# A two-step pipeline, a convolution in 64x64 array tiles, and casts moved between engines, in a fused attention and feed-forward kernel

## The chip, the core and the metric

One core of a Trainium2 chip. The metric is device microseconds of one execution; most executions of a kernel agree within 0.3%, some are 1.5% or more slower and are called slow. The engines are TensorE (PE; PEld is its weight load), VectorE (DVE), ScalarE (ACT), GpSimd (POOL) and SyncE (SP), which issues the transfers. SBUF is the on-chip memory that holds the tiles, PSUM the one that TensorE writes its results to. "Span" is what the profile of one execution covers.

## The reference, cut to what matters

```python
for t in range(S):                                  # B=4, H=8, S=768, D=48
    cur = einsum(u * k_t, v_t)
    y_t = einsum(r_t, state + cur)
    state = w * state + einsum(k_t, v_t)
x = y as (B, S, 384)
gate = sigmoid(sum over 5 taps of conv_w[tap] * shifted x)   # per channel, causal
out = (gate * (x @ w_val)) @ w_out
```

Attention is done in chunks of 128 positions with decays multiplied into k and r beforehand. A **unit** is two chunks (256 positions of one batch), so there are 12 units.

## The kernel before

Each unit goes through: transposes of scaled k and r; `prod` (the product pr of rT and kT on VectorE), `bonus` (a small matmul giving s), scores and mask, state and decay, `bonus_v` (dv = v * s on GpSimd); then the attention output `y_out`, and the feed-forward: `conv`, `value`, `project`. The loop runs them four steps deep:

```python
for i in range(N + 3):
    x, a, y, f = i, i - 1, i - 2, i - 3
    ... loads for x + 3
    if ok(a): prod(a)
    if ok(f): conv(f)
    if ok(x): transp_k(x)
    if ok(a): bonus(a); attn(a, 0); mask_at(a, 0); bonus_v(a); state(a, 0); decay(a, 0)
    if ok(f): value(f)
    if ok(a): attn(a, 1); mask_at(a, 1); state(a, 1); decay(a, 1)
    if ok(y): y_out(y)
    if ok(f): project(f)
    ...  # two of the next batch's r pieces in two steps of three: scale_r on GpSimd, transp_r
    if ok(x + 1) and x > 0: scale_k(x + 1)          # on VectorE
    if ok(x + 1): cast_v(x + 1)                     # two casts on GpSimd
```

The convolution uses full 128x128 diagonal weights, one per tap and per 128 channels:

```python
for Ts in ((0, 1), (2,)):
    g_ps = ps_mm.tile([128, len(Ts), W], F32, name="mm_ps")      # ps_mm: three PSUM buffers
    for i, T in enumerate(Ts):
        for t in range(KW):                                       # 5 taps, W = 256 columns
            nc.tensor.matmul(out=g_ps[:, i, :], lhsT=cwdiag[:, T, t, :],
                             rhs=xT[:, T, t0 + t : t0 + t + W], start=(t == 0), stop=(t == KW - 1))
    nc.scalar.activation(out=gate[...], in_=g_ps, func=AF.Sigmoid)
```

## Time and profile before

| | before |
|---|---|
| time, median of 4 runs | 122.94 us (122.79 to 123.26) |
| span of the profiled run | 123.1 us; that run took 124.88 us, a slow one |
| steps from one attention output to the next, in the steady part | 7.45 us on average |
| TensorE busy between the outputs of units 2 and 9 | 51.8 of 52.2 us |

Lines of the profile give start, duration, engine, line, operation, output and inputs, and in brackets what ended the idle time before. The product pr:

```profile
45.55 0.69 DVE L259 TENSOR_TENSOR pr<-rT,kT 128x1024 bf16<-128x1024 bf16 x1 [2.13 <-ACT rT L222]
52.02 0.68 DVE L259 TENSOR_TENSOR pr<-rT,kT 128x1024 bf16<-128x1024 bf16 x1
59.28 0.99 DVE L259 TENSOR_TENSOR pr<-rT,kT 128x1024 bf16<-128x1024 bf16 x1
```

It takes 0.69 us, once 0.99.

### The profile page before, as it was taken

The page shows a single profiled execution, that of the slowest core. Times are in us where ns is not written, and L with a number is a line of the kernel's source. Part 1 is how long each engine was busy: PE and PEld are TensorE (multiplying, and loading weights), DVE is VectorE, ACT ScalarE, POOL GpSimd, SP SyncE. Part 2 cuts the span into 40 slices and gives each one's busy share as a digit, 9 for nine tenths or more (in the row PEclk, how much of TensorE's full clock was granted, in tenths as well). Part 3 has the DMA queues.
Part 4 walks back from the last instruction along what each step waited for, and adds up shares of the span by engine and source line. Part 5 has one row for each costly group of instructions (what it writes and reads, how often), then busy time and mean ns, then how long its engine had stood idle before and what let it go on. Part 6 is the DMA issues. An engine that isn't in the chain of part 4 may idle for free.

```text
span 123.1 us, 4291 instructions
## 1 busy us (share of the span) xinstructions
PE 100.1 (81%) x1851; PEld 77.7 (63%) x1851; DVE 81.7 (66%) x130; ACT 65.4 (53%) x113; POOL 62.3 (51%) x84
## 2 busy tenths in 40 slices
PE   0035862893589999999999999999999999999950
PEld 0023641672357687886977878787787877778720
DVE  0549669663856938959597695986949787653030
ACT  4599720319033393664938737295691736364730
POOL 6926516592817927039789430995946050500000
PEclk9999999999555799999999999999999999999999
DMA  2999999997999989688499779782030110303213
GB/s 46 166 339 233 193 206 347 242 319 142 221 213 243 326 173 252 136 204 179 141 290 258 183 168 239 151 191 74 5 128 5 61 67 5 128 8 133 74 54 128
DMA packets 58510, 20.54 MB, mean 167 GB/s; under 512 B 50422, under 2 KB 58491, under 8 KB 58491
## 3 DMA queue, kind: packets, MB, share of 16 engines
q1 hardware_dynamic: 58362, 20.26, 67.0%
q8 instruction: 14, 0.23, 0.8%
q0 software_dynamic: 128, 0.00, 0.2%
q14 instruction: 6, 0.04, 0.1%
HBM read 15.54 MB, written 4.72 MB: 165 GB/s over the span
## 4 chain that ended last, share of the span: by engine, by line
PE 63%; SPq 17%; DVE 8%; DMA 5%; issue 2%; ACT 1%; DVEq 0%
PE mm_ps L397 16%; PE mm_ps L359 11%; SPq L72 10%; PE mm_ps L437 10%; PE mm_ps L417 8%; DMA k_st<-in_k_dram 5%; SPq L80 5%; PE at_ps L293 5%; PE tr_ps L246 4%; PE kv_ps L319 3%; DVE cwdiag L197 3%; PE tr_ps L221 3%; DVE at L305 2%; PE kv_ps L328 2%; PE mm_ps L266 2%
## 5 line engine op out<-in xcount | busy, mean ns | idle before, releaser
L279 POOL TENSOR_TENSOR dv<-v_st,s_sb 128x384 bf16<-128x384 f32 x24 | 19.4, 828 | 31.3 <-PE at_ps L293 27.9
L305 DVE TENSOR_TENSOR at<-at_ps,mask 128x1024 bf16<-128x1024 f32 x24 | 29.3, 1220 | 2.6 <-PE at_ps L293 1.6
L387 ACT CAST xT<-mm_ps 128x384 bf16<-128x384 f32 x24 | 11.5, 478 | 31.1 <-PE mm_ps L359 30.4
L397 PE MATMUL mm_ps<-xT,cwdiag 128*128 128x256 bf16 x180 | 23.4, 284 | 1.5 <-DVE cwdiag L197 1.5
L238 POOL CAST vb<-v_st 128x384 bf16<-128x384 f32 x24 | 17.6, 753 | 9.0 <-DMA v_st<-in_v_dram 9.0
L397 PEld LDWEIGHTS <-cwdiag 128*128 128x128 bf16 x180 | 17.6, 100 | 5.5 <-DVE cwdiag L197 2.4
L209 POOL TENSOR_TENSOR rs<-r_st,dr 128x576 bf16<-128x576 f32 x13 | 18.6, 1449 | 3.5 <-DMA r_st<-in_r_dram 3.4
L246 PE MATMUL tr_ps<-ident,ks 128*128 128x128 bf16 x96 | 9.0, 250 | 10.1 <-DVE ks L228 9.9
L425 DVE TENSOR_TENSOR hT<-mm_ps,gate 128x512 bf16<-128x512 f32 (+1 forms) x24 | 12.2, 548 | 7.2 <-PE mm_ps L417 7.2
L249 ACT COPY kT<-tr_ps 128x1024 bf16<-128x1024 bf16 x12 | 12.1, 1012 | 7.8 <-PE tr_ps L246 7.3
L404 ACT ACTIVATE gate<-mm_ps 128x512 bf16<-128x512 f32 (+1 forms) x24 | 11.2, 493 | 8.6 <-PE mm_ps L397 6.8
L228 DVE TENSOR_TENSOR ks<-k_st,dk 128x768 bf16<-128x768 f32 x12 | 13.2, 1098 | 3.5 <-DMA k_st<-in_k_dram 3.5
L417 PE MATMUL mm_ps<-xT,wval 128*128 128x256 bf16 x108 | 14.7, 284 | 0.0
L246 PEld LDWEIGHTS <-ks 128*128 128x128 bf16 x96 | 7.6, 113 | 11.1 <-DVE ks L228 10.6
L437 PE MATMUL mm_ps<-wout,hT 128*128 128x384 bf16 x72 | 13.8, 328 | 0.5 <-DVE hT L425 0.5
L444 ACT COPY o_sb<-mm_ps 128x384 f32<-128x384 f32 x24 | 11.5, 478 | 3.0 <-PE mm_ps L437 1.8
L222 ACT COPY rT<-tr_ps 128x768 bf16<-128x768 bf16 x16 | 12.1, 808 | 0.4 <-PE tr_ps L221 0.4
L293 PE MATMUL at_ps<-rT,kT 48*128 48x128 bf16 x192 | 10.8, 239 | 1.7 <-DVE at L305 1.5
L259 DVE TENSOR_TENSOR pr<-rT,kT 128x1024 bf16<-128x1024 bf16 x12 | 8.8, 735 | 5.0 <-ACT rT L222 5.0
L417 PEld LDWEIGHTS <-wval 128*128 128x128 bf16 x108 | 10.8, 102 | 2.0 <-issue 0.2
L344 DVE TENSOR_TENSOR z<-kv_ps,wcm 128x384 bf16<-128x384 f32 x20 | 10.9, 547 | 0.0
L275 DVE COPY s_sb<-mm_ps 128x16 f32<-128x16 f32 x12 | 2.1, 174 | 12.5 <-issue 5.2
(58 smaller groups left out, 125.6 us busy)
## 6 DMA issues: line engine op xcount, KB each, us to landing
k_st<-in_k_dram SPq DMA_DIRECT2D x24, 192.0 KB, 4.7
r_st<-in_r_dram SPq DMA_DIRECT2D x8, 576.0 KB, 6.2
v_st<-in_v_dram SPq DMA_DIRECT2D x24, 192.0 KB, 4.5
out_dram<-o_sb SPq DMA_DIRECT2D x12, 384.0 KB, 2.6
wv_st<-in_moe_w_val_dram SPq DMA_DIRECT2D x1, 576.0 KB, 4.8
wo_st<-in_moe_w_out_dram SPq DMA_DIRECT2D x1, 576.0 KB, 6.0
w_bc<-in_w_dram SPq DMA_DIRECT2D x1, 192.0 KB, 3.7
wt<-in_w_dram POOLq DMA_DIRECT2D x2, 0.8 KB, 4.5
```

The source lines that it names most:

```text
L72: nc.sync.dma_start(out=d[n][:, cl], in_=src[b, :, t0 : t0 + C, :].transpose([1, 0, 2]))
L209: eng.tensor_tensor(out=rs_t[p][:, :, :, 0:D].rearrange("p j a d -> p a j d"), in0=r_st[b][:, hs, :].rearrange("p a (j d) -> p a j d", d=D ...
L228: nc.vector.tensor_tensor(out=ks_t[n % 3][:, :, :, :, 0:D].rearrange("p c n a d -> p c (n a) d"), in0=k_st[n], in1=dk[:, None, :, :].to_br ...
L238: nc.gpsimd.tensor_copy(heads(vb[:, cl], H), v_st[n][:, cl])
L246: nc.tensor.transpose(tr[:, cl, p, :], ks[:, cl, p].rearrange("p a x -> p (a x)"), ident)
L279: nc.gpsimd.tensor_tensor(out=dv_t[n % 2][:, cl].rearrange("p (h d) -> p h d", d=D), in0=v_st[n][:, cl], in1=st["s", n][:, cl, :, None].to ...
L293: nc.tensor.matmul(out=at_ps[:, par, p, :], lhsT=kT[rows, p, cs], rhs=rT[rows, p, cs], start=(p == 0), stop=(p == NP - 1), skip_group_chec ...
L305: nc.vector.tensor_tensor(out=st["at", n, cl].rearrange("p a n i -> p (a n) i"), in0=st["at_ps", n, cl].rearrange("p a n i -> p (a n) i"), ...
L359: nc.tensor.matmul(out=y_ps[32 * q : 32 * q + 32, T, :], lhsT=lt, rhs=rh, start=q not in first, stop=last, skip_group_check=True,)
L397: nc.tensor.matmul(out=g_ps[:, i, :], lhsT=cwdiag[:, T, t, :], rhs=xT[:, T, t0 + t : t0 + t + W], start=(t == 0), stop=(t == KW - 1),)
L417: nc.tensor.matmul(out=v_ps[:, i, :], lhsT=wval[:, kt, T * 128 : T * 128 + 128], rhs=xT[:, kt, t0 : t0 + W], start=(kt == 0), stop=(kt == ...
L437: nc.tensor.matmul(out=o_ps, lhsT=hT[:, T, cl * C : cl * C + C], rhs=wout[:, T, :], start=(T == 0), stop=(T == NT - 1),)
```

## The change

Intent: shorten the start and the drain of the pipeline (feed-forward one step behind the scores instead of two), cut TensorE's convolution by packing four 64x64 tiles into the array, and take the k scaling off VectorE and the v casts off GpSimd. Its core:

```diff
-    for i in range(N + 3):
-        x, a, y, f = i, i - 1, i - 2, i - 3
+    for i in range(N + 1):
+        f = i - 1
...
+        if ok(f): y_out(f)
+        if ok(i + 1):
+            cast_v(i + 1)                     # now one cast on ScalarE
+            scale_k(i + 1, nc.gpsimd)         # was on VectorE
+        if ok(i):
+            prod(i); attn(i, 0); mask_at(i, 0)
+            bonus(i); bonus_v(i); state(i, 0); decay(i, 0)
+        ... scale_r on GpSimd, one or two pieces
+        if ok(f): conv(f); value(f)
+        if ok(i): attn(i, 1); mask_at(i, 1); state(i, 1); decay(i, 1)
+        ... transp_r, transp_k(i + 1), project(f), transp_r
```

```diff
-                        lhsT=cwdiag[:, T, t, :],
-                        rhs=xT[:, T, t0 + t : t0 + t + W],
+        for T0 in (0, 2):
+            for t in range(KW):
+                for q in range(2):
+                    for i in range(2):
+                        T = 2 if T0 else i
+                        c0, n0, o0 = (i * C, C, W) if T0 else (0, W, 0)
+                        rows = slice(64 * q, 64 * q + 64)
+                        qo = (q + i) % 2
+                        nc.tensor.matmul(
+                            out=g_ps[i][64 * qo : 64 * qo + 64, o0 : o0 + n0],
+                            lhsT=cwdiag[rows, T, t, :],
+                            rhs=xT[rows, T, t0 + c0 + t : t0 + c0 + t + n0], ...)
```

Cut away here: value, projection and weights follow the new layout of the channels; the first batch's r is loaded and scaled ahead of everything (two pieces on GpSimd); 60 warm-up matmuls run ahead; the diagonals are prepared at the end of step 0; the last output goes out in two halves.

More of the change, by code (lines that the diff above doesn't have):

```diff
@@ L77, in load_r @@
         r_st[b] = ldr.tile([128, H, J * D], F32, name="r_st")
-        for hh in range(2):
-            hs = slice(hh * NP, hh * NP + NP)
+        nd = NP if b == 0 else 2
+        for hh in range(nd):
+            hs = slice(hh * (H // nd), (hh + 1) * (H // nd))
             nc.sync.dma_start(
@@ L86 @@
     nc.sync.dma_start(out=w_bc, in_=w.partition_broadcast(128))
-    load_kv(0, "k")
     load_r(0)
+    load_kv(0, "kv")
     load_kv(1, "k")
-    load_kv(0, "v")
-    load_kv(2, "k")
-    load_kv(1, "v")
     nc.scalar.preload_act_table_set("natural_log_exp_and_others")
@@ L172 @@
     wv_st = consts.tile([128, NT, DM], F32)
-    wo_st = consts.tile([128, NT, DM], F32)
+    wo_st = consts.tile([128, 4, DM], F32)
     cw5 = consts.tile([KW, DM], F32)
@@ L178, in load_weights @@
         nc.sync.dma_start(out=wv_st, in_=moe_w_val.rearrange("(t p) n -> p t n", p=128))
-        nc.sync.dma_start(out=wo_st, in_=moe_w_out.rearrange("(t p) n -> p t n", p=128))
-    wval = consts.tile([128, NT, DM], BF16)
-    wout = consts.tile([128, NT, DM], BF16)
+        wo = moe_w_out.rearrange("(t p) n -> p t n", p=128)
+        nc.sync.dma_start(out=wo_st[:, 0::2, :], in_=wo[:, 0::2, :])
+        nc.sync.dma_start(out=wo_st[64:128, 1::2, :], in_=wo[0:64, 1:3, :])
+        nc.sync.dma_start(out=wo_st[0:64, 1::2, :], in_=wo[64:128, 1:3, :])
+    wval = consts.tile([128, NT, 4, 128], BF16)
+    wout = consts.tile([128, 4, DM], BF16)
     cw5b = consts.tile([KW, DM], BF16)
     cwT = consts.tile([128, NT, KW], F32)
-    cwdiag = consts.tile([128, NT, KW, 128], BF16)
+    cwdiag = consts.tile([128, NT, KW, 64], BF16)
+    eye = consts.tile([128, 64], BF16)
     def prep_conv():
@@ L194, in prep_conv, with cast_weights @@
         nc.vector.tensor_copy(cwT, cw_ps[:, :, 0:KW])
-    def prep_diag(T):
-        nc.vector.tensor_tensor(
-            out=cwdiag[:, T],
-            in0=ident[:, None, :].to_broadcast([128, KW, 128]),
-            in1=cwT[:, T, :, None].to_broadcast([128, KW, 128]),
-            op=ALU.mult,
-        )
+        for q in range(2):
+            rows = slice(64 * q, 64 * q + 64)
+            nc.vector.tensor_copy(eye[rows], ident[rows, rows])
+        for T in range(NT):
+            nc.vector.tensor_tensor(
+                out=cwdiag[:, T],
+                in0=eye[:, None, :].to_broadcast([128, KW, 64]),
+                in1=cwT[:, T, :, None].to_broadcast([128, KW, 64]),
+                op=ALU.mult,
+            )
+    def cast_weights():
+        wv = wv_st.rearrange("p k (t x) -> p k t x", x=128)
+        nc.gpsimd.tensor_copy(wval[:, :, 0::2, :], wv[:, :, 0::2, :])
+        nc.gpsimd.tensor_copy(wval[:, :, 1::2, 64:128], wv[:, :, 1:3, 0:64])
+        nc.gpsimd.tensor_copy(wval[:, :, 1::2, 0:64], wv[:, :, 1:3, 64:128])
+        nc.scalar.copy(out=wout, in_=wo_st)
     st = {}
@@ L214, in scale_r, with transp_r @@
         )
-    def transp_r(b, p):
+    def transp_r(b, p, dve=False):
         if p == 0:
@@ L221, in transp_r @@
             nc.tensor.transpose(tr[:, j, :], rs_t[p][:, j].rearrange("p a x -> p (a x)"), ident)
-        nc.scalar.copy(
+        (nc.vector.tensor_copy if dve else nc.scalar.copy)(
             out=st["rT", b][:, p, :].rearrange("x (p j) -> x p j", j=J),
@@ L225, in transp_r, with scale_k @@
         )
-    def scale_k(n):
-        nc.vector.tensor_tensor(
+    def scale_k(n, eng):
+        eng.tensor_tensor(
             out=ks_t[n % 3][:, :, :, :, 0:D].rearrange("p c n a d -> p c (n a) d"),
@@ L236, in cast_v @@
         vb = vb_t[n % 4]
-        for cl in range(U):
-            nc.gpsimd.tensor_copy(heads(vb[:, cl], H), v_st[n][:, cl])
+        nc.scalar.copy(
+            out=vb[:, :, 16 : 16 + 64 * H].rearrange("p c (h x) -> p c h x", x=64)[:, :, :, 0:D],
+            in_=v_st[n],
+        )
     def transp_k(n):
@@ L277, in bonus_v @@
     def bonus_v(n):
-        for cl in range(U):
-            nc.gpsimd.tensor_tensor(
-                out=dv_t[n % 2][:, cl].rearrange("p (h d) -> p h d", d=D),
-                in0=v_st[n][:, cl],
-                in1=st["s", n][:, cl, :, None].to_broadcast([128, H, D]),
-                op=ALU.mult,
-            )
+        nc.gpsimd.tensor_tensor(
+            out=dv_t[n % 2].rearrange("p c (h d) -> p (c h) d", d=D),
+            in0=v_st[n].rearrange("p c h d -> p (c h) d"),
+            in1=st["s", n].rearrange("p c h -> p (c h)")[:, :, None].to_broadcast([128, U * H, D]),
+            op=ALU.mult,
+        )
     def attn(n, cl):
@@ L391, in conv @@
         xT, t0 = xT_t[b % 2], cu * W
-        gate = ffn.tile([128, NT, W], BF16, name="gate")
-        for Ts in ((0, 1), (2,)):
-            g_ps = ps_mm.tile([128, len(Ts), W], F32, name="mm_ps")
-            for i, T in enumerate(Ts):
-                for t in range(KW):
-                    nc.tensor.matmul(
-                        out=g_ps[:, i, :],
-                        lhsT=cwdiag[:, T, t, :],
-                        rhs=xT[:, T, t0 + t : t0 + t + W],
-                        start=(t == 0),
-                        stop=(t == KW - 1),
-                    )
-            nc.scalar.activation(
-                out=gate[:, Ts[0] : Ts[-1] + 1, :], in_=g_ps, func=AF.Sigmoid
-            )
+        gate = ffn.tile([128, 2, W + C], BF16, name="gate")
+        g_ps = [ps_mm.tile([128, W + C], F32, name="mm_ps") for i in range(2)]
+        for T0 in (0, 2):
+            for t in range(KW):
+                for q in range(2):
+                    for i in range(2):
+                        T = 2 if T0 else i
+                        c0, n0, o0 = (i * C, C, W) if T0 else (0, W, 0)
+                        rows = slice(64 * q, 64 * q + 64)
+                        qo = (q + i) % 2
+                        nc.tensor.matmul(
+                            out=g_ps[i][64 * qo : 64 * qo + 64, o0 : o0 + n0],
+                            lhsT=cwdiag[rows, T, t, :],
+                            rhs=xT[rows, T, t0 + c0 + t : t0 + c0 + t + n0],
+                            start=(t == 0 and T0 == 0),
+                            stop=(t == KW - 1),
+                            skip_group_check=True,
+                        )
+        for i in range(2):
+            nc.scalar.activation(out=gate[:, i], in_=g_ps[i], func=AF.Sigmoid)
         st["gate", n] = gate
@@ L411, in value @@
         xT, t0 = xT_t[b % 2], PAD + cu * W
-        hT = ffn.tile([128, NT, W], BF16, name="hT")
-        for Ts in ((0, 1), (2,)):
-            v_ps = ps_mm.tile([128, len(Ts), W], F32, name="mm_ps")
-            for i, T in enumerate(Ts):
-                for kt in range(NT):
-                    nc.tensor.matmul(
-                        out=v_ps[:, i, :],
-                        lhsT=wval[:, kt, T * 128 : T * 128 + 128],
-                        rhs=xT[:, kt, t0 : t0 + W],
-                        start=(kt == 0),
-                        stop=(kt == NT - 1),
-                    )
-            ts = slice(Ts[0], Ts[-1] + 1)
+        hT = ffn.tile([128, 2, W + C], BF16, name="hT")
+        for i in range(2):
+            v_ps = ps_mm.tile([128, W + C], F32, name="mm_ps")
+            for kt in range(NT):
+                nc.tensor.matmul(
+                    out=v_ps[:, 0:W],
+                    lhsT=wval[:, kt, i, :],
+                    rhs=xT[:, kt, t0 : t0 + W],
+                    start=(kt == 0),
+                    stop=(kt == NT - 1),
+                    skip_group_check=True,
+                )
+            for kt in range(NT):
+                nc.tensor.matmul(
+                    out=v_ps[:, W : W + C],
+                    lhsT=wval[:, kt, 2 + i, :],
+                    rhs=xT[:, kt, t0 + i * C : t0 + i * C + C],
+                    start=False,
+                    stop=(kt == NT - 1),
+                    skip_group_check=True,
+                )
             nc.vector.tensor_tensor(
-                out=hT[:, ts, :], in0=v_ps, in1=st["gate", n][:, ts, :], op=ALU.mult
+                out=hT[:, i], in0=v_ps, in1=st["gate", n][:, i], op=ALU.mult
             )
@@ L435, in project @@
             o_ps = ps_mm.tile([128, DM], F32, name="mm_ps")
-            for T in range(NT):
+            for j, (i, c0) in enumerate(((0, cl * C), (1, cl * C), (cl, W))):
                 nc.tensor.matmul(
                     out=o_ps,
-                    lhsT=hT[:, T, cl * C : cl * C + C],
-                    rhs=wout[:, T, :],
-                    start=(T == 0),
-                    stop=(T == NT - 1),
+                    lhsT=hT[:, i, c0 : c0 + C],
+                    rhs=wout[:, 2 + cl if j == 2 else i, :],
+                    start=(j == 0),
+                    stop=(j == 2),
                 )
             nc.scalar.copy(out=o_sb[:, cl, :], in_=o_ps)
-        nc.sync.dma_start(
-            out=out[b, cu * W : cu * W + W, :].rearrange("(c p) n -> p c n", p=128),
-            in_=o_sb,
-        )
+            if n == N - 1:
+                t0 = cu * W + cl * C
+                nc.sync.dma_start(out=out[b, t0 : t0 + C, :], in_=o_sb[:, cl, :])
+        if n < N - 1:
+            nc.sync.dma_start(
+                out=out[b, cu * W : cu * W + W, :].rearrange("(c p) n -> p c n", p=128),
+                in_=o_sb,
+            )
     def ok(n):
@@ L455 @@
     load_weights()
-    load_kv(2, "v")
-    scale_k(0)
-    for p in range(NP):
-        scale_r(0, p, nc.gpsimd if p == 2 else nc.vector)
+    load_kv(1, "v")
+    load_kv(2, "k")
+    warm = ps_mm.tile([128, 128], F32, name="mm_ps")
+    for _ in range(60):
+        nc.tensor.matmul(out=warm, lhsT=ident, rhs=ident, start=True, stop=True)
+    for p in range(NP):
+        scale_r(0, p, nc.gpsimd if p % 2 else nc.vector)
+    scale_k(0, nc.vector)
+    for p in range(2):
+        transp_r(0, p)
+    transp_k(0)
+    for p in range(2, NP):
+        transp_r(0, p, dve=True)
+    cast_v(0)
     for par in range(2):
@@ L466 @@
         nc.vector.tensor_copy(wcm[rows, :, par, :], wct[rows, :, None].to_broadcast([64, NP, D]))
-    scale_k(1)
-    cast_v(0)
-    for i in range(N + 3):
-        x, a, y, f = i, i - 1, i - 2, i - 3
-        if x % NU == 0 and x // NU + 1 < B:
-            load_r(x // NU + 1)
-        if ok(x + 3):
-            load_kv(x + 3, "kv")
-        if ok(a):
-            prod(a)
+    for i in range(N + 1):
+        f = i - 1
+        if i == 0:
+            load_kv(2, "v")
+            load_r(1)
+        if i % NU == 2 and i // NU + 2 < B:
+            load_r(i // NU + 2)
+        if ok(i + 3):
+            load_kv(i + 3, "kv")
+        if ok(f):
+            y_out(f)
+        if ok(i + 1):
+            cast_v(i + 1)
+            scale_k(i + 1, nc.gpsimd)
+        if ok(i):
+            prod(i)
+            attn(i, 0)
+            mask_at(i, 0)
+            bonus(i)
+            bonus_v(i)
+            state(i, 0)
+            decay(i, 0)
+        rb = i // NU + 1
+        sp, tp = ((0,), ()) if i % NU == 0 else ((1, 2), (0, 1)) if i % NU == 1 else ((3,), (2, 3))
+        if i < NU:
+            sp = tp
+        if rb < B:
+            for p in sp:
+                scale_r(rb, p, nc.gpsimd)
@@ L478 @@
         if ok(f):
             conv(f)
-        if ok(x):
-            transp_k(x)
-        if x == 0:
-            for p in range(NP):
-                transp_r(0, p)
-        if ok(a):
-            bonus(a)
-            attn(a, 0)
-            mask_at(a, 0)
-            bonus_v(a)
-            state(a, 0)
-            decay(a, 0)
-        if ok(f):
-            value(f)
-        if ok(a):
-            attn(a, 1)
-            mask_at(a, 1)
-            state(a, 1)
-            decay(a, 1)
-        if ok(y):
-            y_out(y)
+            value(f)
@@ L501 @@
+        if ok(i):
+            attn(i, 1)
+            mask_at(i, 1)
+            state(i, 1)
+            decay(i, 1)
+        if rb < B and tp:
+            transp_r(rb, tp[0])
+        if ok(i + 1):
+            transp_k(i + 1)
         if ok(f):
             project(f)
-        rb, rp = {0: (x // NU, (2, 3)), 1: (B, ()), 2: (x // NU + 1, (0, 1))}[x % NU]
-        if 0 < rb < B:
-            for p in rp:
-                scale_r(rb, p, nc.gpsimd)
-                transp_r(rb, p)
-        if ok(x + 1) and x > 0:
-            scale_k(x + 1)
@@ L511 @@
-        if ok(x + 1):
-            cast_v(x + 1)
-        if i == 2:
+        if rb < B and tp:
+            transp_r(rb, tp[1])
+        if i == 0:
             prep_conv()
-            nc.gpsimd.tensor_copy(wval, wv_st)
-            for T in range(NT):
-                prep_diag(T)
-            nc.scalar.copy(out=wout, in_=wo_st)
+            cast_weights()
 _INS = ['r', 'k', 'v', 'w', 'u', 'moe_w_val', 'moe_conv_w', 'moe_w_out']
```

## The prediction

> **What bounds the kernel now.** I read the page's busy shares and 40 slices first, then the stretches table (busy time of each engine per window), then the time line of TensorE in the steady part, and last the DMA waits.
>
> ```profile
> PE 100.1 (81%) x1851; PEld 77.7 (63%) x1851; DVE 81.7 (66%) x130; ACT 65.4 (53%) x113; POOL 62.3 (51%) x84
> ...
> PE   0035862893589999999999999999999999999950
> ...
> PEclk9999999999555799999999999999999999999999
> DMA  2999999997999989688499779782030110303213
> ```
>
> TensorE is full from slice 13 (40 us) to the end; before that it is half idle while the DMA row stands at 9. So there are two stages: a filling stage of some 40 us and a steady stage that TensorE sets. The stretches confirm it (start:end and length, then busy us of each engine, granted clock, DMA share, GB/s):
>
> ```profile
> 12.00:26.00 14.00, 9.24 (x101) 6.50 (x103) 10.54 (x17) 4.37 (x6) 7.63 (x12) 1.00 1.02 259
> 26.00:41.00 15.00, 11.24 (x145) 7.95 (x144) 9.28 (x14) 5.45 (x8) 8.91 (x9) 0.67 1.02 222
> ...
> 57.00:101.00 44.00, 43.67 (x893) 35.15 (x882) 35.25 (x51) 28.44 (x50) 28.71 (x32) 1.00 0.56 142
> ```
>
> From 57 to 101 us TensorE is busy 43.67 of 44 us, VectorE 80%, ScalarE and GpSimd 65%. One unit (256 positions of one batch; there are 12) takes 7.5 us there: the attention output of successive units starts at 56.4, 63.6, 71.7 and 78.9. What the 7.5 us are made of, from the starts in the time line (start, busy us, engine, line, operation):
>
> ```profile
> 71.67 0.35 PE L359 MATMUL mm_ps<-rT,z 128*32 128x128 bf16 x12
> ...
> 72.90 1.15 PE L437 MATMUL mm_ps<-wout,hT 128*128 128x384 bf16 x6
> 73.89 1.81 PE L397 MATMUL mm_ps<-xT,cwdiag 128*128 128x256 bf16 x15
> 75.53 0.61 PE L246 MATMUL tr_ps<-ident,ks 128*128 128x128 bf16 x8
> 75.98 0.34 PE L266 MATMUL mm_ps<-uw,pr 128*128 128x2 bf16 x8
> 76.25 0.40 PE L293 MATMUL at_ps<-rT,kT 48*128 48x128 bf16 x8
> ```
>
> Start to next start: attention output 1.23 (80 matmuls), projection 0.99, convolution 1.64 (15), k transposes 0.45, bonus 0.27, scores 0.33; likewise value 0.98, a second score block 0.33, two state blocks 0.35 each, r transposes 0.67 in two units of three (0.45 on average). Sum 7.4, against 7.5 measured: no bubble worth naming, so the steady stage shrinks only by the matmuls taken away.
>
> The filling stage hangs on loads:
>
> ```profile
> 29.80 0.96 DVE L228 TENSOR_TENSOR ks<-k_st,dk 128x768 bf16<-128x768 f32 x1 [2.80 <-DMA k_st<-in_k_dram]
> ```
>
> This is k of unit 3. The first convolution (unit 0) stands behind it in program order: it runs at 35 us.
>
> **What the Trainium skill says.** (1) "TensorEngine Tiling (Array Packing)", Tiling Modes and Restrictions: a 64x64 mode makes four independent tiles, a mode change drains the array, and column tiling switches the fast weight load off. The trace of before has 128x32 tiles in the attention output: 80 load-and-multiply pairs in 1.23 us, 15 ns each, where a lone 128-column matmul takes 56 ns (transposes, 0.45 over 8). So packing works here, and a 32-column weight load fits in 14 ns. (2) "PSUM — Partial Sum Buffer", PSUM bank collisions: quoting a guide, different row tiles cannot write one bank at the same time, while its measured case of a collision is one bank and one quadrant. The new convolution lets both row halves write one bank in different halves of the partitions; no run yet shows what that costs. (3) "GPSIMD Engine Reference", 4.1: two-input elementwise work is about twice as slow as on VectorE, one-input work about equal. The trace agrees: the 128x576 product takes 0.76 us on VectorE and 1.41 on GpSimd. (4) "TensorE: Matmul & The Clock Gate", Part 1: the clock is released after some 3.4 us of sustained work. The trace agrees roughly: 0.5 is recorded from 31 to 40 us, and the first conv matmuls at 35 us ran 250 ns apart against 109 later.
>
> **The change, part by part.**
>
> Convolution. 15 matmuls of 256 columns become 20 of 256 and 20 of 128 on 64x64 tiles, four at a time. If packed, the moving side takes 20 x 107/4 + 20 x 53/4 = 0.80 us. Weight loads: 40 of 64 columns, twice the 14 ns seen for 32, 40 x 28 = 1.1 us if they go one after the other. I take 1.05 us for 1.64: 0.6 less per unit, 7 us in all. Value and projection stream as many columns as before (value 6 x 256 + 6 x 128 = 2304 = 9 x 256).
>
> Steady unit. 7.4 - 0.6 = 6.8 us. One new wait: there are still three PSUM buffers for these groups, and the second value group takes the first gate's buffer, free only after the 0.49 us sigmoid that begins once the whole convolution is done: about +0.2. The output copy that feeds the convolution now lies within one step: it needs about 0.75 us after the attention output, and scores, bonus and state (0.95) cover it. I take 6.9 to 7.0 us.
>
> Other engines per unit (durations from the groups). ScalarE: two xT 0.96, v cast 0.83 (768 elements at the 1.01 ns of the wout cast plus start), two gates 0.98, kT 1.01, two o_sb 0.96, rT 4/3 x 0.81 = 1.08: 5.8. VectorE loses the k scaling (1.1): masks 2.44, z 1.09, hT 1.1, pr 0.74, s 0.17: 5.5. GpSimd: bonus-v 1.65, r scaling 4/3 x 1.41 = 1.9, k scaling 768 elements at 2.2 to 2.45 ns = 1.75; less the casts (1.5): 5.3, and 6.2 in a unit with two r pieces. All below 6.9, but at 77 to 85%.
>
> Depth. Steps fall from 15 to 13: the feed-forward of unit n runs one step after its scores, no longer two after. At the step that starts when k of unit 3 has come, before ran the convolution of unit 0; after runs that of unit 2. Two units of feed-forward (2 x 3.6 us) move into time in which TensorE now waits for loads.
>
> Filling stage. DMA amount and packets are unchanged and the queue is full, so arrivals follow bytes. In before, 3.3 MB had landed by 18.6 us, 4.9 by 23, 6.9 by 31.7. In the new order that puts k1 at 13, weights at 17, v1 18.5, k2 20.3, v2 22.3, first half of r1 24.5, k3 28.5, v3 31. r1 and GpSimd's strict order then lead: scaling of r1 pieces 0, 1 to 27.5, k3 to 30.3, bonus-v of unit 2 to 32.6, r1 pieces 2, 3 to 35.5. TensorE has their transposes at the end of step 2, so step 3 starts at about **36 us**. The 60 warm-up matmuls run while nothing else could; they are free and may keep the clock up for a while.
>
> Tail. From the start of the last step: attention output 1.23, copy 0.75, convolution 1.05, value with the gate wait 1.1, hT 0.6, projection 0.99 with its copy 0.6, and 3.4 us from the last copy to the end as in before (119.7 to 123.1): 9.8.
>
> Sum: 36 + 9 x 6.9 + 9.8 = **107.9**, rounded down to 107.5 because single waits in the first stage are taken at their worst.
>
> **Rivals.** (a) DMA becomes the bound. Queue time is 67% of 123 us = 82 us, 6.5 per unit, hardly less than the new 6.9. For: the DMA row is full up to 46 us. Against: with loads three units ahead, k11 lands near 78 us by my byte count and is wanted near 90. If it binds: 104 to 112. (b) GpSimd or ScalarE becomes the bound or, through their strict order, makes TensorE wait at the r transposes: GpSimd runs k scaling, bonus-v (behind the s copy), r scaling in a row, to about 6.4 us after the step's start, just when TensorE wants the last transpose. With contention from VectorE (the casts took 0.51 to 1.24 us) a unit would take 7.4: 112. (c) The 64x64 matmuls don't overlap: two at a time gives 1.6 us and 113; none gives 3.2 us, 9 us a unit, 127. The 15 ns pairs of the attention output speak against it. (d) The filling stage is shorter (step 3 at 31, when v3 lands) and the unit at 6.7: 101.
>
> **Range and chances.** Most of the gain (some 8 of 15 us) comes from depth, about 6 from the convolution. Between (d) and (b, c) the range is 101 to 114. Same or slower needs a unit of over 8.2 us, thus (c) at its worst or two rivals together: 5%.
>
> **What the new profile would show.** Convolution near 26 ns from start to start (wrong if over 40); attention outputs 6.9 us apart; step 3's attention output near 36 us, ahead of it a wait for GpSimd's r scaling; TensorE at about 90% busy between 40 and 98 us, GpSimd and ScalarE 75 to 85%; DMA share near 78%, with waits for loads only in the first 36 us. It is wrong if TensorE waits more than 0.5 us per unit for GpSimd or ScalarE in the steady part, if loads still end its waits after 45 us, or if the clock stays at 0.5 past 40 us.

## The result, and the profile after

| | before | after |
|---|---|---|
| time, median of 4 runs | 122.94 us | 118.97 us (118.70 to 120.81) |
| ratio | | 0.9666, 95% interval 0.9636 to 0.9697 |

Ratios here are the mean time of one kernel's fast runs over that of the other's in the same rounds, so they are not quite the ratio of the medians. The change is faster, by 3.3%: 4 us, where some 15 were predicted.

The page of the changed kernel, the lines that answer to those of before:

```profile
PE 94.5 (81%) x2247; PEld 73.7 (63%) x2247; DVE 76.9 (66%) x122; ACT 69.3 (59%) x123; POOL 65.2 (56%) x62
...
PE   0395273875999698999979799999898999999860
...
PEclk9999955578599999999999999999999999999999
DMA  0899999999979898997879997994894003030303
```

and the stretches (start:end and length, then busy us of TensorE, its weight loads, VectorE, ScalarE, GpSimd; granted clock, DMA share, GB/s):

```profile
12.00:26.00 14.00, 8.41 (x144) 6.40 (x141) 11.75 (x20) 6.42 (x9) 8.29 (x7) 0.63 1.05 215
26.00:41.00 15.00, 12.30 (x271) 9.71 (x272) 10.53 (x17) 7.25 (x14) 9.41 (x8) 0.89 0.99 252
...
57.00:101.00 44.00, 41.32 (x1087) 32.15 (x1085) 33.16 (x46) 30.09 (x56) 26.70 (x18) 1.00 0.66 161
```

TensorE has less to do, but is no longer full: 41.3 of 44 us between 57 and 101 us, where it had 43.7. The convolution itself did what was hoped. From the time line of TensorE in one step (start, busy time, engine, line, operation; the next start tells the length):

```profile
72.38 0.41 PE L374 MATMUL mm_ps<-at,vb 128*32 128x128 bf16 x16
...
73.63 0.40 PE L308 MATMUL at_ps<-rT,kT 48*128 48x128 bf16 x8
74.25 0.35 PE L282 MATMUL mm_ps<-uw,pr 128*128 128x2 bf16 x8 [0.23 <-ACT xT L402]
74.47 0.33 PE L334 MATMUL kv_ps<-vb,ks 128*128 128x96 bf16 x4
74.64 0.33 PE L343 MATMUL kv_ps<-z,ident 128*128 128x384 bf16 x1
74.89 1.02 PE L418 MATMUL mm_ps<-xT,cwdiag 64*64 64x256 bf16 x40
75.85 0.50 PE L437 MATMUL mm_ps<-xT,wval 128*128 128x256 bf16 x3
```

Forty tiled matmuls take 0.96 us (74.89 to 75.85), 24 ns each, instead of 1.64 us for fifteen. Value then takes 1.24 us instead of 0.98: its second group waits for a buffer that the first gate frees, as predicted. So TensorE is relieved of 0.68 - 0.26 = 0.4 us per unit: between the outputs of units 2 and 9 it is busy 48.6 of 51.8 us, 6.94 us per step, where before had 51.8 of 52.2. And yet the steady step is 7.40 us against 7.45. What TensorE waited for, in the whole run (waiter, its line, waited for; us in total, times, longest):

```profile
PE mm_ps L282 <- DVE pr L275: 5.4, 6, 2.1
...
PE tr_ps L262 <- DVE ks L242: 2.2, 1, 2.2
PE tr_ps L235 <- POOL rs L223: 1.7, 2, 1.0
```

The bonus matmuls (L282) wait for the product pr. Of these 5.4 us only 2.3 lie between the outputs of units 2 and 9, 0.32 us per step; the other idle time there is one standstill of 0.66 us, for which the trace shows no wait, and 0.23 us for xT. Here is pr on VectorE beside k's scaling on GpSimd, from the time lines of both, in two steps:

```profile
72.56 1.64 DVE L275 TENSOR_TENSOR pr<-rT,kT 128x1024 bf16<-128x1024 bf16 x1
80.04 2.00 DVE L275 TENSOR_TENSOR pr<-rT,kT 128x1024 bf16<-128x1024 bf16 x1 [0.63 <-ACT kT L265]
```

```profile
71.82 1.83 POOL L242 TENSOR_TENSOR ks<-k_st,dk 128x768 bf16<-128x768 f32 x1
...
79.67 1.83 POOL L242 TENSOR_TENSOR ks<-k_st,dk 128x768 bf16<-128x768 f32 x1
```

pr has its operands and has begun, but ends at 74.20 and 82.04, each time 0.54 to 0.55 us after GpSimd's scaling (73.65 and 81.50), although it does not read what GpSimd writes. Alone it takes 0.69. The masks, which read one operand from PSUM, take 1.21 to 1.23 us whatever GpSimd does.

Where the steps lie (start of the attention output of unit 2; mean of the seven steps from there to unit 9; units 9 to 11; the rest to the end of the span):

| | unit 2 at | mean step | units 9 to 11 | rest |
|---|---|---|---|---|
| before (a slow run) | 49.2 | 7.45 | 11.1 | 10.6 |
| after | 42.9 | 7.40 | 12.7 | 9.4 |

After is 6.3 us ahead at unit 2, gains next to nothing for seven units, and gives 1.6 us back in the last two: before has the scores of one unit left there and no transposes of k, after the scores of two and the transposes of one. The profiled run of before took 1.9 us longer than its fast median, and where it lost them isn't known, so any of these differences may be smaller by up to that much.

### The profile page after: what moved, and what is told of

It reads as the page before. It is cut to its first block, busy times and chain, and to the rows that moved or that the text cites. A ratio compares the mean times of both kernels' runs of the same rounds, so it can differ in the third digit from the quotient of the medians.

```text
span 116.8 us, 5086 instructions
## 1 busy us (share of the span) xinstructions
PE 94.5 (81%) x2247; PEld 73.7 (63%) x2247; DVE 76.9 (66%) x122; ACT 69.3 (59%) x123; POOL 65.2 (56%) x62
## 4 chain that ended last, share of the span: by engine, by line
PE 41%; SPq 16%; issue 12%; DVE 10%; ACT 8%; POOL 6%; DMA 3%; DVEq 0%; POOLq 0%; ACTq 0%
SPq L72 12%; PE mm_ps L418 8%; PE mm_ps L374 7%; PE mm_ps L437 6%; PE mm_ps L466 5%; DVE pr L275 5%; ACT kT L265 4%; DMA k_st<-in_k_dram 3%; POOL ks L242 3%; DVE hT L454 3%; PE at_ps L308 3%; PE mm_ps L282 3%; POOL rs L223 2%; PE kv_ps L334 2%; PE mm_ps L446 2%
## 5 line engine op out<-in xcount | busy, mean ns | idle before, releaser
L294 POOL TENSOR_TENSOR dv<-v_st,s_sb 128x768 bf16<-128x768 f32 x12 | 17.7, 1476 | 35.2 <-DVE s_sb L291 35.2
L454 DVE TENSOR_TENSOR hT<-mm_ps,gate 128x384 bf16<-128x384 f32 x24 | 13.4, 557 | 12.4 <-PE mm_ps L446 11.6
L242 POOL TENSOR_TENSOR ks<-k_st,dk 128x768 bf16<-128x768 f32 x11 | 20.1, 1831 | 1.4 <-DMA k_st<-in_k_dram 1.4
L427 ACT ACTIVATE gate<-mm_ps 128x384 bf16<-128x384 f32 x24 | 10.5, 488 | 12.0 <-PE mm_ps L418 12.0
L251 ACT CAST vb<-v_st 128x768 bf16<-128x768 f32 x12 | 10.3, 860 | 5.9 <-DMA v_st<-in_v_dram 5.9
L418 PE MATMUL mm_ps<-xT,cwdiag 64*64 64x256 bf16 (+1 forms) x480 | 12.9, 252 | 0.7 <-ACT xT L402 0.6
L418 PEld LDWEIGHTS <-cwdiag 64*64 64x64 bf16 x480 | 11.0, 110 | 2.6 <-issue 2.1
L235 PE MATMUL tr_ps<-ident,rs 128*128 128x128 bf16 x96 | 8.6, 230 | 2.9 <-POOL rs L223 1.7
L374 PE MATMUL mm_ps<-at,vb 128*32 128x128 bf16 x384 | 10.1, 227 | 0.0
L235 PEld LDWEIGHTS <-rs 128*128 128x128 bf16 x96 | 6.7, 103 | 4.7 <-POOL rs L223 2.0
```

What stands on the lines that cost most here:

```text
L235: nc.tensor.transpose(tr[:, j, :], rs_t[p][:, j].rearrange("p a x -> p (a x)"), ident)
L242: eng.tensor_tensor(out=ks_t[n % 3][:, :, :, :, 0:D].rearrange("p c n a d -> p c (n a) d"), in0=k_st[n], in1=dk[:, None, :, :].to_broadcas ...
L294: nc.gpsimd.tensor_tensor(out=dv_t[n % 2].rearrange("p c (h d) -> p (c h) d", d=D), in0=v_st[n].rearrange("p c h d -> p (c h) d"), in1=st[ ...
L374: nc.tensor.matmul(out=y_ps[32 * q : 32 * q + 32, T, :], lhsT=lt, rhs=rh, start=q not in first, stop=last, skip_group_check=True,)
L418: nc.tensor.matmul(out=g_ps[i][64 * qo : 64 * qo + 64, o0 : o0 + n0], lhsT=cwdiag[rows, T, t, :], rhs=xT[rows, T, t0 + c0 + t : t0 + c0 + ...
L454: nc.vector.tensor_tensor(out=hT[:, i], in0=v_ps, in1=st["gate", n][:, i], op=ALU.mult)
```

## The experiments

**Theory A**: VectorE and GpSimd hold each other up. While GpSimd runs, a VectorE instruction with both operands in SBUF stands still; and the work hangs in a ring: pr, bonus, copy of s, bonus-v (GpSimd), r and k scaling (GpSimd), which hold up the next pr. **Theory B**: TensorE still sets the step, since the tiles cost more than counted. **Theory C**: late loads lead the filling stage.

**One word: k scaling back on VectorE.**

```diff
-            scale_k(i + 1, nc.gpsimd)
+            scale_k(i + 1, nc.vector)
```

> The changed kernel with the k scaling put back on VectorE (one word). Theory A (VectorE's product pr of two SBUF operands stands still while GpSimd scales k, and bonus, s, bonus-v and the next r and k scaling hang behind it in a ring): pr takes 0.69 us in every step instead of up to 2.2, TensorE's waits for pr (5.4 us) fall below 2 us, a step between attention outputs falls from 7.4 to about 7.0 us, time 114 to 116.5 us. Theory B (TensorE itself still sets the 7.4 us, because the 64x64 tiles and the shorter value matmuls cost more than I counted): step unchanged, time 118 to 120 us. Theory C (loads): unchanged, 118 to 120 us, with waits for k loads.

Measured: 118.84 us median, 117.02 to 119.33; three of four runs were slow. The trace (of a slow run) tells what was asked: pr took 0.68 or 0.69 us in all twelve units, the step fell to 7.27, not to 7.0. TensorE's waits for pr fell from 5.4 to 4.0 us, not below 2; in the steady part they fell from 2.3 to 1.0 us. The lines of pr at the step in question and k's scaling ahead of it, both on VectorE:

```profile
80.49 1.35 DVE L242 TENSOR_TENSOR ks<-k_st,dk 128x768 bf16<-128x768 f32 x1
81.76 0.68 DVE L275 TENSOR_TENSOR pr<-rT,kT 128x1024 bf16<-128x1024 bf16 x1
```

Theory A's mechanism holds: now k's scaling is the one held (1.35 us, 0.95 alone) by GpSimd's r scaling, less long. The gain expected of it was too large for two reasons that the trace shows: the waits left in the steady part (0.50 us, twice) are for a pr that itself waits for rT from ScalarE, and in the setup k of unit 1 now stands ahead of pr of unit 0 on VectorE, which began at 19.7 instead of 18.5 us. (Unit 2's output came at 44.4 us; but this run took 2.3 us longer than the fast one, so that isn't to be laid to the edit.)

**The bonus and the copy of s ahead of the mask.**

```diff
-            mask_at(i, 0)
             bonus(i)
+            mask_at(i, 0)
```

> The changed kernel with the bonus and the copy of s ahead of the first mask in VectorE's order, so that GpSimd's bonus-v may start some 1.2 us earlier in each step. Theory A (the ring pr, s, bonus-v, r scaling, k scaling, pr): k scaling ends earlier, pr is held less, the step falls by 0.2 to 0.4 us, time 115.5 to 117.5 us. Theory B or C: 118 to 120 us; slightly slower if the later mask delays the second score block.

Measured: 117.46 us (117.38 to 117.66), all fast, ratio 0.9532 (0.9501 to 0.9563): 1.3 points better than after. The step fell from 7.40 to 7.22; pr's longest durations fell from 2.2 to 1.5 us. No work was removed, no engine relieved, no load moved: only VectorE's order changed, so that GpSimd starts earlier. That supports the ring and speaks against C, and against B as a full account. Its share is 0.18 us of the step.

**The convolution alone, on the kernel before** (its conv, value, projection and weights replaced by those of after).

> The kernel before with the 64x64 convolution (and the value, projection and weight layout that go with it) alone; four-step pipeline, casts and scalings as before. In the kernel before TensorE has no gaps, so if the convolution saves TensorE what its trace shows (0.69 us per unit, less 0.26 us for the shorter value matmuls) the time falls by 12 x 0.43 = 5 us at least and 8 at most: 115 to 118 us, thus the convolution alone gives as much as the whole change, and the rest of the change gives nothing. If the 64x64 tiles cost elsewhere (mode changes, slower neighbours): 121 to 123 us.

Measured: 122.13 us median (120.71 to 123.13), ratio 0.9831 (0.9767 to 0.9895), verdict unclear. A miss: the convolution took 0.95 us there too, but only some 2 us of the expected 5 came out. In its trace (a slow run) TensorE waits 3.2 us for GpSimd's r scaling, and GpSimd itself waits 9.7 us for v and 4.3 us for r to be loaded. With v's casts moved to ScalarE besides:

```diff
-        for cl in range(U):
-            nc.gpsimd.tensor_copy(heads(vb[:, cl], H), v_st[n][:, cl])
+        nc.scalar.copy(out=vb[...], in_=v_st[n])
```

> The kernel before (four steps deep) with the tiled convolution, as in the run of the convolution alone (122.1 us), and the v casts on ScalarE besides. In that run TensorE waited 3.2 us for GpSimd's r scaling, which stood behind the casts. If GpSimd's order is what kept the convolution from paying in the deep pipeline, the waits go and the time falls to 117.5 to 120 us, with a step of 7.0 to 7.1 us. If the loads' arrival (the r of the next batch, the v of the next unit) is it: 121 to 122.5 us.

Measured: 122.30 us median, one fast run of 118.66 and three slow ones from 122.1 to 122.7. The profiled fast run has steps of 6.7 to 6.8 us in two of three units and 8.0 to 8.5 in the third. What a deep pipeline with this convolution is worth stays open: its states lie 3% apart.

**Load order: k of unit 2 and v of unit 1 ahead of the weights.**

```diff
-    load_weights()
-    load_kv(1, "v")
     load_kv(2, "k")
+    load_kv(1, "v")
+    load_weights()
```

> The changed kernel with k of unit 2 and v of unit 1 loaded ahead of the weights. If the late k of unit 2 (landed at 24.2 us) leads the filling stage, its scaling starts near 19 us, the third step's attention output moves from 42.9 to some 39 to 40 us, and the time falls to 115 to 117 us. If GpSimd's order and VectorE's convolution preparation lead it, or the weights then come late, it stays at 118 to 120 us.

Measured: 119.82 us (119.07 to 120.73), ratio 0.9724 (0.9664 to 0.9785), no better than after; unit 2 came at 44.8 instead of 42.9 us. Either the load of k was not what led, or the weights, which now came later, took its place; the runs without loads, below, decide between the two.

**The tiled convolution undone, the rest of the change kept.**

> The changed kernel with the full-array convolution, value and projection of the kernel before: the tiled convolution undone alone. If TensorE set the steady step, the step would grow by what the convolution and value cost it more: 0.69 - 0.26 = 0.43 us, some 5 us in all, time 123 to 124 us. If a ring through VectorE and GpSimd sets it (theory A), a part hides beside the waits: 120 to 122 us.

Measured: 124.28 us (123.89 to 125.06), ratio 1.0069 (0.998 to 1.0158), the same as before. So pipeline, casts, scaling and warm-up together are worth nothing, and within this pipeline the convolution is worth 4 points of the ratio, 5 us. For theory A this was a miss: it had forecast 120 to 122 us, and 123 to 124 if TensorE set the step. The step grew by 0.28 us (7.68) where TensorE has 0.41 us more to do (51.5 us busy in seven steps, against 48.6): two thirds of TensorE's work show, one third hides beside the waits. So theory B is wrong in its reason, since the tiles cost no more than counted, but TensorE still fills 94% of the changed kernel's step, and the ring adds the waits on top. The undone kernel's unit 2 comes at 43.7 us, 5.5 ahead of before, and all of that is given back: 7 x 0.23 in the steps, 2.4 in the last two units (13.6 against 11.1 us), and 1.5 by which the profiled run of before, a slow one, had the longer span (123.1 against 121.6).

**Setup scaling all on VectorE.**

```diff
-        scale_r(0, p, nc.gpsimd if p % 2 else nc.vector)
+        scale_r(0, p, nc.vector)
```

> The changed kernel with all four r pieces of the first batch scaled on VectorE (two on GpSimd in the changed kernel), nothing else. In the changed kernel the two r scalings on VectorE took 2.6 us instead of 1.5 and k's 2.15 instead of 0.95, all beside GpSimd's. If they hold each other up (theory A), without GpSimd they take 0.76 and 0.95 each, and pr of the first unit starts 0.5 to 1 us earlier (18.5 us in the changed kernel); time 0.3 to 1 us less, if no load leads there. If VectorE is simply slower on these shapes (rival), four pieces take 5 us and the time grows by 1 us.

Measured: 118.62 us median, one fast run of 116.73, three slow. In the trace pr of unit 0 began at 17.7 instead of 18.5 us. In after, this is the setup on VectorE and GpSimd, from the time line:

```profile
9.60 2.63 DVE L223 TENSOR_TENSOR rs<-r_st,dr 128x576 bf16<-128x576 f32 x2 [3.75 <-ACT dr L132]
9.65 3.84 POOL L223 TENSOR_TENSOR rs<-r_st,dr 128x576 bf16<-128x576 f32 x2 [2.58 <-ACT wct L136]
12.15 2.15 DVE L242 TENSOR_TENSOR ks<-k_st,dk 128x768 bf16<-128x768 f32 x1
```

Two r pieces on each engine and k were through at 14.3 us; in the combined kernel below, VectorE alone does four r pieces in 2.77 us and k in 0.95. The help of the second engine cost more than it gave.

**The diagonals prepared on ScalarE, before the loop** (fifteen small scaled copies there instead of VectorE's work at the end of step 0).

> The changed kernel with the preparation of the convolution's diagonals taken from VectorE, where it stands ahead of pr of unit 1, to ScalarE before the loop. Theory A: in the changed kernel it took VectorE 4.3 us (the three products 2.9 us beside GpSimd's k scaling, 1.3 alone), pr of unit 1 began at 26.9 us and TensorE waited 2.1 us for it; without it that pr starts at 25 us or before, the third step's attention output moves 1.5 to 2.5 us forward from 42.9, time 116.5 to 117.5 us. If loads (k of unit 2, at 24.2 us) lead the filling stage, less than 0.5 us comes of it.

Measured: 118.38 us median, one fast run of 116.09, three slow. The trace shows why little came of it: pr of unit 1 did begin at 24.7 instead of 26.9 us, but took 2.01 us, held by GpSimd's k scaling. The wait had only moved.

**All four together.**

> k scaling on VectorE, s before the mask, setup scaling on VectorE, diagonals on ScalarE, all on the changed kernel. If the ring and the shared way of VectorE and GpSimd are what ate the gain, the effects add: steady step 7.1 us, third step's attention output at 39 to 40 us, time 112.5 to 115 us. If each only moves the wait (rival), it stays over 116 us.

Measured: 115.04 us (114.67 to 115.67), all fast, ratio 0.9306 (0.9237 to 0.9374). It is correct and faster than both kernels. Unit 2 comes at 40.1 us, the step is 7.21, pr takes 0.68 to 0.69 us in every unit. Its page:

```profile
PE 93.1 (83%) x2247; PEld 72.4 (64%) x2247; DVE 77.3 (69%) x128; ACT 73.7 (65%) x142; POOL 41.5 (37%) x49
...
PE   0397362787799889999999899999998999999750
```

GpSimd has a third less to do than in after, VectorE hardly more (77.3 against 76.9 us), because what was moved back no longer stands waiting. The step was expected at 7.1 us and the time at 115 us at most, so the expectation was met but for the last tenths. That each edit alone only moves the wait, the rival, is out. That the parts simply add isn't shown, since three of the four have one fast run each. Nor is all of the earlier unit 2 (40.1 for 42.9) the engines': here the clock was full again from 25 us, not from 32, and convolution and value of unit 0 took 2.2 us (26.8 to 29.0) where they had taken 3.6 (28.25 to 31.85). Up to 1.4 of the 2.7 us may be the clock's; no run separates the two. With pr never held, TensorE still waits 0.50 us for it once per batch, and there pr waits for rT.

**Without the warm-up, and with r's second transpose ahead of the projection**, both on the combined kernel.

> The combined kernel (115.0 us) with one warm-up matmul instead of 60. If the warm-up is worth something, the r and k transposes of the setup (0.50 us for six in the combined kernel, 0.80 in the kernel before) run at half clock and step 0 starts 0.5 to 1 us later: 115.5 to 116.5 us. If loads and the copies after the transposes lead there anyway, the clock having fallen back by 14 us in any case: 114.5 to 115.5 us, no difference.

> The combined kernel with the second r transpose of a step ahead of the projection instead of after it, so that ScalarE copies rT before the two output copies. If the wait for rT at the first unit of each batch (pr waits 1.4 us for it, TensorE some 0.5 us for pr) matters: 0.5 to 1.5 us less, 113.5 to 114.5 us. If GpSimd's r scaling then comes too late for it: the same or up to 1 us more.

Measured: 116.12 us with ratio 0.9283 (0.9188 to 0.9378) and 116.31 us with ratio 0.9315 (0.9229 to 0.9402), against 0.9306. No difference for either. The warm-up did raise the clock: the transposes of the setup ran 55 to 60 ns apart with it and 107 without. But by 14.3 us half clock was back, until 24.6; without the warm-up it lasted until 25.9 us. The second brought "the same", but not for the reason named: pr's waits for rT fell from 4.4 to 2.1 us, and TensorE waited 2.6 us instead at r's transposes, for buffers that ScalarE's copies free.

**Loads left out** (wrong result: units 1 and 2 use k and v of unit 0).

```diff
+            if n in (1, 2):
+                d[n] = d[0]
+                continue
```

> Wrong result on purpose: the changed kernel with the same two units' loads left out. If the late loads are what made its filling stage 7 us longer than I predicted: the third step's attention output moves from 42.9 to 37 us, time 112 to 114 us. If the ring through VectorE and GpSimd leads it (theory A), the loads give 1 to 2 us at most: 40.5 us or later, time 116.5 to 118 us.

> Wrong result on purpose: the combined kernel (115.0 us) in which units 1 and 2 take unit 0's k and v, so 1.6 MB fewer are loaded in the first 35 us and the rest lands 6 to 7 us earlier. If loads now lead the filling stage (theory C, my 36 us were right for the engines), the third step's attention output moves from 40.1 to 36 to 37 us and the time to 111 to 112.5 us. If the engines' chains and the half clock lead it, it stays at 39 us or more, time over 114 us.

Measured: on the changed kernel 118.82 us (118.60 to 119.44), ratio 0.966, unit 2 at 42.5 us: 1.6 MB less to load in the filling stage, and nothing gained, not even the 1 to 2 us that I had left to loads. The first half of batch 1's r landed at 20.7 instead of 28.3 us, and its scaling still began at 29.9 us (30.3 in after). Theory C falls for the changed kernel; the engines' chains lead. On the combined kernel 112.76 us (112.45 to 113.70), ratio 0.9172, unit 2 at 38.6 instead of 40.1: once the chains are loosened, these loads are worth 1.3 points, less than I expected. What fills the rest of the way to 36 us isn't shown.

## Why the prediction was wrong

Its sum was 36 + 9 x 6.9 + 9.8 = 107.9. Measured, in the same terms: 42.9 for the start of step 3, 64.5 for the nine steps (7.16 each), 9.4 for the tail, 116.8 of span, and 1.9 us from span to time: 118.7, the time of the profiled run.

- **The filling stage, "step 3 starts at about 36 us": 6.9 us short, the main error.** The chain was named rightly: every link (r1 pieces 0, 1; k3; bonus-v of unit 2; r1 pieces 2, 3) came in the predicted order, but they ended at 33.1, 34.8, 39.3 and 42.0 us where I had 27.5, 30.3, 32.6 and 35.5. From the time line of GpSimd:

```profile
30.29 2.77 POOL L223 TENSOR_TENSOR rs<-r_st,dr 128x576 bf16<-128x576 f32 x2
33.00 1.83 POOL L242 TENSOR_TENSOR ks<-k_st,dk 128x768 bf16<-128x768 f32 x1
37.78 1.48 POOL L294 TENSOR_TENSOR dv<-v_st,s_sb 128x768 bf16<-128x768 f32 x1 [2.94 <-DVE s_sb L291]
39.21 2.76 POOL L223 TENSOR_TENSOR rs<-r_st,dr 128x576 bf16<-128x576 f32 x2
```

  The instructions took about what I had reckoned. The chain began 5.8 us late (30.3 for 24.5), won back 1 us where it needn't wait for k3, and lost 2.1 where bonus-v of unit 2 waited 2.9 us for s. I had let loads time it. These were late too (k2 landed at 23.5 us for 20.3, the first half of r1 at 28.3 for 24.5), but that was hidden: leaving loads out changed nothing. What timed the chain was the setup (pr of unit 0 only at 18.5 us, after scalings that held each other up) and step 1 (bonus-v of unit 1 at 28.9 us, behind a pr that stood behind the diagonals on VectorE, which took 2.9 us beside k's scaling and 1.3 without). From the first attention output (23.2) to the third (42.9) part of TensorE's work also ran at half clock: the clock row shows 5 to 8 from 15 to 32 us. How the 6.9 us divide among these stays open; the combined edit took 2.7 of them away, the clock's part of that included.
- **"Two units of feed-forward move into time in which TensorE now waits for loads", 7 us: given back.** The undone convolution shows that depth and moves together give nothing. The work did move in; that the third step began later for that reason isn't shown. And the drain of the deep pipeline, which I had not weighed, is not idle: its last steps are only shorter.
- **Convolution, 1.05 us: right, and a little pessimistic** (0.96). Packing works with both row halves in one PSUM bank. The gate's wait of 0.2 us was right (0.26 in all). That the convolution would be worth about 6 us was nearly right (5).
- **The steady step, 6.9 to 7.0: measured 7.40 up to unit 9; over all nine steps 2.4 us short.** TensorE's own sum was right: it is busy 6.94 us per step. The term that failed is "other engines, all below 6.9". I added up durations taken from before and asked whether each engine has room. The trouble is not occupancy (GpSimd was busy 34.7 of 51.8 us in this part) but that VectorE's pr and GpSimd's scaling exclude each other. Of the 0.45 us by which the step is longer than TensorE's work, 0.32 are waits for pr. With the mutual hold lessened or gone (the second experiment, the combined kernel) the step is 7.2, not 6.9: so about 0.2 us of it are the hold, and the rest is pr waiting for rT and the standstill. My rival (b) had contention lengthening GpSimd's work and delaying r's transposes, to 7.4 us. That the size fits is luck: in this part GpSimd's instructions kept their length (k's scaling 1.81 to 1.84 us), VectorE's was lengthened, and TensorE never waited for r's transposes. In before it also went the other way: casts that began behind VectorE's k scaling took 1.23 us instead of 0.50.
- **Rival (a), DMA as the bound: rightly set aside.** Rival (c), tiles that don't overlap: did not happen.
- **Span for time: 1.9 us.** The profiled run of before was a slow one, so its span (123.1) happened to equal the median time of the fast runs (122.9). I predicted a span and called it a time.
- **Slips in the working, without weight in the result.** 82 us of queue time over 12 units is 6.9 us each, not 6.5; the tail's terms sum to 9.7, not 9.8. The first convolution began at 32.4 us, not 35, and its matmuls ran 213 ns apart (median): the 250 is an average with a wait for the diagonals in it. And half clock was not confined to 31 to 40 us: the clock row shows 9 up to the first change that it records (27.7 us in before), but the transposes before that are 107 ns apart, those just after it 56. Read the spacing beside the row.

The SBUF mechanism is in the Trainium skill, "SBUF — State Buffer", section "SBUF: two separate sides", which I had not drawn on: GpSimd and VectorE share a pair of ports as an exclusive lock held for a whole instruction, and a VectorE instruction with two SBUF inputs needs it against a GpSimd one that reads SBUF. Traces agree: in the four steps of after in which pr is held it ends 0.54 to 0.55 us after GpSimd's instruction, the masks with a PSUM operand are never longer than 1.23 us, and with k's scaling gone from GpSimd pr is 0.69 us throughout.

## What to carry to other kernels

Before moving an elementwise instruction from one engine to another, list what else runs at that moment on the two engines and whether they share a way to memory: summed busy times will say there is room where two instructions in fact take turns. A shorter matmul only pays in full if nothing else forms a ring of nearly the same length (here 0.28 of 0.41 us showed in the step), so walk once around each loop of engine orders (here pr, s, dv, r, k, pr) and add it up. And a shallower pipeline moves work into the start; it is worth nothing if the start is led by a serial chain and the old drain was busy.

## What the Trainium skill lacked or had wrong

- "TensorEngine Tiling (Array Packing)", Gotcha 1, reads as if row tiles could never share a PSUM bank. Here two row tiles write one bank at a time, in different halves of its partitions: 40 matmuls in 0.96 us, 24 ns each, results correct. "PSUM — Partial Sum Buffer" has the finer rule, by bank and quadrant.
- "GPSIMD Engine Reference", 4.1, gives the cost of moving work to GpSimd as GpSimd's own slowness (about two; here 1.83 against 0.95 us for k's scaling). What it costs VectorE meanwhile, which stands on the SBUF page, can be larger: in four of twelve units pr took 1.38 to 2.23 us instead of 0.69.
- "SBUF — State Buffer" has the lock, but no figure for how long a two-input VectorE instruction still takes after the release. Here 0.54 to 0.55 us of pr's 0.69 remain after GpSimd's instruction ends.
- No page has it: in 12 of 13 profiled runs with 2187 or more matmuls TensorE stood still once or twice, for 0.2 to 1.3 us in the steady part, with no wait that the trace shows (the combined kernel alone had none), and not in the two with 1851 and 1911. The packed traces show one thing beside it: each of the 15 standstills ended 2.3 to 2.8 us after the start of a 16 KB transfer of the queue that section 3 of the page lists as "q8 instruction". So late instructions are the likely cause; no run tests it.
